# GELU in one ScalarE activation and a second layernorm's rstd on GpSimd, in a gated mix of a long convolution and an MLP mixer

## The chip, the core and the metric

One core of a Trainium2 chip runs the whole program. The metric is the device time of one launch in microseconds (us), from the first to the last instruction and what lies around them; lower is better. PE is the matmul engine (TensorE), PEld its weight loads, ACT is ScalarE, DVE is VectorE, POOL is GpSimd, SP is the engine that here only issues DMAs.

## The reference, cut to what matters

```
x = A_q                                            # 2048 x 640
g = sigmoid((x * gate_w).sum(-1))
a = q * (causal long convolution of kv with ssm_k, by FFT) # kv: 4-tap filter of k, times v
h  = gelu(layernorm(x) @ w1)                       # tanh form, 2048 x 640
hs = (h with its four column groups shifted by 1, -1, 2, -2 rows) @ w2
x1 = x + hs
b  = x1 + gelu(layernorm(x1) @ w3) @ w4            # w3: 640 x 1536, w4: 1536 x 640
out = g * a + (1 - g) * b
```

The GELU is `gelu(x, approximate=True)`, that is x * sigmoid(1.5957691 * (x + 0.044715 x^3)).

## The kernel before, in words

Every operation is recorded by hand in program order (`P.op`, `P.dma`); a small recorder works out from the named reads and writes of each operation which semaphores it must wait for, also on an earlier operation of its own engine (PE's writes excepted). Each engine runs its operations in exactly the order in which the code records them. A helper, `pipeline(stages, n)`, records n items through several stages with the later stages first in each step, so item t is in stage s while item t+1 is in stage s-1.

The program goes through these parts, the times being those of the profiled execution:

- **Loading and first layernorm** (0 to 110 us). 16 tiles of 128 rows: k, v and q are read on SP's queue, DVE makes kv, ACT and DVE make the layernorm, DMA transposes write `xT`. Then 16 gate columns, where ACT's sigmoid (L581) and DVE alternate.
- **mm1, the product with w1** (110 to 157 us, `mm1_s0` at L613). 20 items: 4 chunks of 512 rows, 5 column groups each. An item is 5 matmuls 128x128 by 512 columns into one of the four PSUM banks of `PB` (L619), followed by the GELU of `gelu_stages` (L589): a square on ACT (L595), a multiply-add on DVE (L598), a sigmoid on ACT (L602), a product on DVE (L624). In the fifth item of each chunk the last product is four DVE instructions of 32 partitions each (L637), since each row group lands at another shift. A bank is free for the item four later when the last product has read it.
- **mm2, the product with w2, and the second layernorm** (157 to 209 us, `mm2_s0` at L664). 16 tiles of 128 rows: 10 matmuls of 320 columns, then DVE adds the residual (L686), takes the statistics (L502, L503, L504), ACT takes a square root (L506), DVE the reciprocal (L510), minus mean times rstd (L511) and the normalised tile (L515). SP writes x1 to a scratch tensor, reads the next q and transposes the tile. DVE's order in a step is `ln_dve` of the tile before, then L686 and the statistics of this one; so what follows L504 on DVE is L510 of the same tile.
- **Forward DFT and its pointwise products** (202 to 357 us). Eight units; a unit is 48 matmuls for the filter and kv (L773), evacuated by 24 ACT copies (L776), and then some 27 DVE products (L819 to L835) of about 16 us. The units on PE and ACT run ahead of DVE as far as buffers go.
- **mm3 and mm4** (340 to 479 us). Four chunks of 512 rows. mm3: 12 items of 5 matmuls by 512 columns (L854) into the four banks of `PA`, each with the same GELU; its last product (L860) writes `uT`. mm4: 4 tiles of 24 matmuls by 320 columns (L887), each closed by a DVE instruction (L897). With each tile a row tile of x1 is read back from the scratch tensor and scaled on ACT (L840) for the tile three later.
- **Inverse DFT and output** (479 to 544 us): 448 matmuls of 320 columns (L947), ACT and DVE behind them.

The weights w3 and w4 are loaded by two DMAs of POOL's queue, recorded behind mm2 (L704, L705).

```
    pipeline([mm1_s0, mm1_s1, mm1_s2, mm1_s3, mm1_s4], len(mm1_items))
...
    pipeline([mm2_s0, mm2_s1, mm2_s2, mm2_s3], NT)
```

Of the kernel before, what the change touches and what calls it, by code (L numbers as in the profile page):

```python
# [8 lines left out]
ACTF = mybir.ActivationFunctionType  # L9
ALU = mybir.AluOpType  # L10
# [221 lines left out]
def bass_gated_mix__ssm_conv_h3__mixer_s_mlp__prompt_kernel(  # L232
# [2 lines left out]
    S, D, F = 2048, 640, 1536  # L235
    NT, DC, FC = 16, 5, 12
    T, BLK, NB, NJ = 1024, 512, 4, 4
    GELU_C1 = 0.044715
    GELU_C2 = 1.5957691216057308
    SQC1 = float(np.sqrt(GELU_C1))  # L240

    P = Prog(nc, pools={"sp": ("sp", 20), "sp_out": ("sp", 3), "sp_scr": ("sp", 3), "act": ("act", 8),
                        "pool": ("pool", 8)})
# [57 lines left out]
    oXrel = alloc(3 * 640)  # L301
    oX1rot = alloc(3 * 640)
    oX1rel = alloc(3 * 640)
    oGel = alloc(3 * 3 * 512)
    oJunk = alloc(2 * 640)
    oXn = alloc(3 * 640)
    oQ = oXrel
# [47 lines left out]
    hTv = V(oHT, 5 * HT_W).rearrange("p (c s) -> p c s", c=5)  # L355
# [12 lines left out]
    xrel = [V(oXrel + i * 640, 640) for i in range(3)]  # L368
    x1rot = [V(oX1rot + i * 640, 640) for i in range(3)]
    x1rel = [V(oX1rel + i * 640, 640) for i in range(3)]  # L370
    gel = [[V(oGel + (s * 3 + i) * 512, 512) for i in range(3)] for s in range(3)]
    junk = [V(oJunk + i * 640, 640) for i in range(2)]
    xn = [V(oXn + i * 640, 640) for i in range(3)]
    qt = [V(oQ + i * 640, 640) for i in range(2)]
# [189 lines left out]
    def st2(t):  # L564
# [4 lines left out]
         r=["taps", "Drow"], w=["taps"])  # L569

    GB = 3
    for t in range(NT):
        for c in range(DC):
            P.op("pe", lambda e, t=t, c=c: e.matmul(bankA(GB)[:, t:t + 1], xT[:, c, t * 128:(t + 1) * 128],  # L574
                                                   gwT[:, c:c + 1], start=(c == 0), stop=(c == DC - 1)),
                 r=[("xT", t), "gwT"], w=["gateps", ("bankA", GB)])
    P.op("dve", lambda e: e.tensor_scalar(gsum[:, 1:2], gsum[:, 0:1], -1.0, None, op0=ALU.mult), r=["gsum"], w=["gsum"])
    for t in range(NT):
        P.op("dve", lambda e, t=t: e.tensor_tensor(gcol(t, 2), scol(0, t, 8), gsum[:, 1:2], ALU.mult),
             r=[("stat", 0, t), "gsum"], w=[("gc", t)])  # L580
        P.op("act", lambda e, t=t: e.activation(gcol(t, 0), bankA(GB)[:, t:t + 1], ACTF.Sigmoid,  # L581
                                                bias=gcol(t, 2), scale=scol(0, t, 5)),
             r=["gateps", ("bankA", GB), ("gc", t), ("stat", 0, t)], w=[("gc", t)])
        P.op("dve", lambda e, t=t: e.tensor_scalar(gcol(t, 1), gcol(t, 0), -1.0, 1.0, op0=ALU.mult, op1=ALU.add),
             r=[("gc", t)], w=[("gc", t)])

    gslot = [0]

    def gelu_stages(ps_ap, key_ps, dst_fn):  # L589
        slot = gslot[0] % 3  # L590
        gslot[0] += 1
        sq, z, sg = gel[slot]

        def a1():
            P.op("act", lambda e: e.activation(sq, ps_ap, ACTF.Square, scale=SQC1), r=[key_ps], w=[("gel", slot, 1)])  # L595

        def d1():
            P.op("dve", lambda e: e.scalar_tensor_tensor(out=z, in0=sq, scalar=1.0, in1=ps_ap, op0=ALU.add, op1=ALU.mult),  # L598
                 r=[("gel", slot, 1), key_ps], w=[("gel", slot, 2)])

        def a2():
            P.op("act", lambda e: e.activation(sg, z, ACTF.Sigmoid, scale=GELU_C2), r=[("gel", slot, 2)], w=[("gel", slot, 3)])  # L602

        def d2():
            for (fn, wk) in dst_fn(sg, ps_ap):
                P.op("dve", fn, r=[("gel", slot, 3), key_ps], w=wk)
        return (a1, d1, a2, d2)

    SHIFT = [1, -1, 2, -2]
    mm1_items = [(sc, ft) for sc in range(4) for ft in range(5)]  # L610
    mm1_g = {}

    def mm1_s0(k):  # L613
        sc, ft = mm1_items[k]
        bb = k % 4
        psb = bankB(bb)
        for c in range(DC):
            lhsT = w1v[:, c, 160 * ft:160 * ft + 128] if ft < 4 else w1t4v[:, c, :]
            P.op("pe", lambda e, lhsT=lhsT, c=c, sc=sc, psb=psb: e.matmul(  # L619
                psb, lhsT, xT[:, c, sc * 512:(sc + 1) * 512], start=(c == 0), stop=(c == DC - 1)),  # L620
                 r=["w1"] + [("xT", 4 * sc + i) for i in range(4)], w=[("bankB", bb)])
        if ft < 4:
            def dst_fn(sg, ps_ap, ft=ft, sc=sc):
                return [(lambda e: e.tensor_tensor(hTv[:, ft, 2 + sc * 512:2 + (sc + 1) * 512], sg, ps_ap, ALU.mult),  # L624
                         [("hT", ft, sc)])]
        else:
            offs = ((0, 3), (32, 1), (64, 4), (96, 0))
            wkeys = [("hT", 4, sc)]
# [5 lines left out]
            def dst_fn(sg, ps_ap, sc=sc, wkeys=wkeys):
                lst = []
                for p0, co in offs:
                    lst.append((lambda e, p0=p0, co=co: e.tensor_tensor(  # L637
                        hTv[p0:p0 + 32, 4, co + sc * 512:co + (sc + 1) * 512], sg[p0:p0 + 32, :],
                        ps_ap[p0:p0 + 32, :], ALU.mult), wkeys))
                return lst  # L640
# [5 lines left out]
    def mm1_s2(k):
        mm1_g[k][1]()

    def mm1_s3(k):
        mm1_g[k][2]()  # L650

    def mm1_s4(k):
        mm1_g[k][3]()
# [189 lines left out]
    mm3_g = {}  # L843

    def emit_mm3(sc):
        ub = sc % 2
        uT = uTv[ub]

        def s0(ft):
            k = sc * FC + ft  # L850
            b = k % 4
            psb = bankA(b)
            for c in range(DC):
                P.op("pe", lambda e, psb=psb, c=c, ft=ft: e.matmul(  # L854
                    psb, w3v[:, c, ft * 128:(ft + 1) * 128], xT[:, c, sc * 512:(sc + 1) * 512],
                    start=(c == 0), stop=(c == DC - 1)),
                     r=["w3"] + [("xT", 4 * sc + i) for i in range(4)], w=[("bankA", b)])
# [8 lines left out]
        def s2(ft):
            mm3_g[sc * FC + ft][1]()

        def s3(ft):
            mm3_g[sc * FC + ft][2]()  # L870

        def s4(ft):
            mm3_g[sc * FC + ft][3]()
# [129 lines left out]
```

## Time and profile before

| | us |
|---|---|
| median of 3 runs | 545.34 |
| lowest and highest | 542.97, 547.1 |
| span of the profiled execution, first to last instruction | 544.1 |
| busy: PE, DVE, ACT, POOL | 313.8, 364.8, 213.6, 15.8 |

The profiled execution has no own total beside its span; the median lies 1.2 us above that span, well inside the spread of the three runs. Busy times are sums over the span: no engine is busy all of it, and which one limits changes from part to part, so the parts are read one by one below.

### The profile page before, as it was taken

How to read it: one execution, taken by the hardware profiler on the slowest of the kernel's cores; microseconds unless marked ns; L12 is line 12 of the kernel's file. 1: busy time of each engine (PE TensorE's matmuls, PEld its weight loads, DVE VectorE, ACT ScalarE, POOL GpSimd, SP SyncE). 2: the span in 40 equal slices, each digit the busy share in tenths (PEclk: the TensorE clock that was granted, in tenths of full speed). 3: DMA queues.
4: the chain of work that ended last, by engine and by line, in shares of the span. 5: the costliest groups of instructions: out<-in, count | busy, mean ns of one | idle time of the engine just before them, and what ended most of it. 6: DMA issues, size and time to landing. Idle time of an engine off the chain costs nothing.

```text
span 544.1 us, 5685 instructions
## 1 busy us (share of the span) xinstructions
PE 313.8 (58%) x1809; PEld 173.1 (32%) x1819; DVE 364.8 (67%) x775; ACT 213.6 (39%) x436; POOL 15.8 (3%) x28
## 2 busy tenths in 40 slices
PE   1000000047664467994267406368789798899996
PEld 0000000012232233552123102125445363577774
DVE  1657858738988884999999993985482937432222
ACT  2555434366630004771233204354563818321111
POOL 3110100010000000000000000000000000000000
PEclk9999999997989997998588756769999999999999
DMA  6599999880016663000000000040101010122221
GB/s 185 113 216 270 299 245 260 196 302 0 1 40 156 154 136 96 2 0 1 1 0 0 0 0 2 0 154 14 36 1 48 2 37 12 37 72 74 84 79 56
DMA packets 59114, 46.01 MB, mean 85 GB/s; under 512 B 35136, under 2 KB 57662, under 8 KB 58830
## 3 DMA queue, kind: packets, MB, share of 16 engines
q1 hardware_dynamic: 36062, 31.46, 21.7%
q10 hardware_dynamic: 21152, 5.25, 6.0%
q0 software_dynamic: 1872, 8.96, 4.9%
q8 instruction: 14, 0.23, 0.2%
q14 instruction: 14, 0.11, 0.1%
HBM read 32.54 MB, written 5.24 MB: 69 GB/s over the span
## 4 chain that ended last, share of the span: by engine, by line
DVE 48%; PE 26%; DMA 11%; issue 6%; ACT 5%; SPq 2%; POOL 0%; DVEq 0%; ACTq 0%; POOLq 0%
PE PA L947 11%; PE PB L887 9%; DMA arena<-in_A_k_dram 9%; DVE arena L835 9%; DVE arena L832 7%; DVE arena L860 5%; DVE arena L598 4%; PE PA L773 3%; DVE arena L686 2%; SPq L125 2%; DVE arena L637 2%; PE PB L619 2%; DVE arena L502 1%; DVE arena L503 1%; DVE arena L822 1%
## 5 line engine op out<-in xcount | busy, mean ns | idle before, releaser
L773 PE MATMUL PA<-arena 128*128 128x512 bf16 (+1 forms) x384 | 80.7, 377 | 57.6 <-ACT arena L776 57.6
L776 ACT ACTIVATE arena<-PA 128x512 bf16<-128x512 f32 (+1 forms) x96 | 50.5, 526 | 81.8 <-DVE arena L832 60.6
L773 PEld LDWEIGHTS PA<-arena 128*128 128x128 bf16 x384 | 40.3, 106 | 97.8 <-ACT arena L776 61.4
L854 PE MATMUL PA<-arena 128*128 128x512 bf16 x232 | 56.9, 391 | 23.0 <-DVE arena L860 22.1
L947 PE MATMUL PA<-arena 128*128 128x320 bf16 x448 | 61.0, 299 | 0.0
L887 PE MATMUL PB<-arena 128*128 128x320 bf16 x384 | 54.3, 299 | 5.5 <-DVE arena L860 5.5
L574 PE MATMUL PA<-arena 128*128 128x1 bf16 x80 | 4.7, 169 | 90.3 <-DMA arena<-arena 90.3
L602 ACT ACTIVATE arena<-arena 128x512 bf16<-128x512 bf16 x68 | 42.4, 623 | 21.3 <-DVE arena L598 21.3
L835 DVE TENSOR_TENSOR arena<-arena 128x960 bf16<-128x960 bf16 (+2 forms) x96 | 47.2, 492 | 3.3
L947 PEld LDWEIGHTS PA<-arena 128*128 128x128 bf16 x448 | 43.8, 98 | 17.0
L832 DVE TENSOR_TENSOR arena<-arena 128x960 bf16<-128x960 bf16 (+2 forms) x96 | 46.6, 486 | 0.0
L887 PEld LDWEIGHTS PB<-arena 128*128 128x128 bf16 x384 | 37.2, 98 | 22.5 <-DVE arena L860 7.9
L598 DVE SCALAR_TENSOR_TENSOR arena<-arena,PA 128x512 bf16<-128x512 bf16 x48 | 32.4, 683 | 12.9 <-ACT arena L595 12.9
L854 PEld LDWEIGHTS PA<-arena 128*128 128x128 bf16 x240 | 22.1, 99 | 57.1 <-ACT arena L595 32.8
L677 PE MATMUL PB<-arena 128*128 128x320 bf16 x160 | 24.6, 300 | 25.0 <-DVE arena L686 22.1
L897 DVE SCALAR_TENSOR_TENSOR arena<-PB,arena 128x640 bf16<-128x640 f32 x16 | 14.1, 884 | 36.6 <-PE PB L887 36.6
L962 DVE TENSOR_TENSOR arena<-arena 128x640 bf16<-128x640 bf16 x16 | 7.9, 493 | 45.5 <-ACT arena L956 45.5
L619 PE MATMUL PB<-arena 128*128 128x512 bf16 x98 | 29.2, 454 | 12.7 <-DVE arena L624 6.2
L956 ACT ACTIVATE arena<-PA,arena 128x640 bf16<-128x640 f32 x16 | 12.7, 794 | 54.7 <-PE PA L947 54.7
L860 DVE TENSOR_TENSOR arena<-arena,PA 128x512 bf16<-128x512 bf16 x48 | 32.7, 682 | 0.8
L574 PEld LDWEIGHTS PA<-arena 128*128 128x128 bf16 x80 | 3.4, 106 | 91.6 <-DMA arena<-arena 91.6
L840 ACT ACTIVATE arena<-arena 128x640 bf16<-128x640 bf16 x16 | 13.0, 826 | 45.9 <-DMA arena<-x_scratch 45.9
(88 smaller groups left out, 364.2 us busy)
## 6 DMA issues: line engine op xcount, KB each, us to landing
arena<-in_A_k_dram SPq DMA_DIRECT2D x61, 160.0 KB, 6.2
arena<-in_A_q_dram SPq DMA_DIRECT2D x48, 160.0 KB, 2.6
arena<-in_B_w_dram POOLq DMA_DIRECT2D x2, 1920.0 KB, 10.8
arena<-in_A_v_dram SPq DMA_DIRECT2D x16, 160.0 KB, 6.8
x_scratch<-arena SPq DMA_DIRECT2D x16, 160.0 KB, 1.8
arena<-x_scratch SPq DMA_DIRECT2D x16, 160.0 KB, 2.2
out_dram<-arena SPq DMA_DIRECT2D x16, 160.0 KB, 1.8
arena<-cG POOLq DMA_DIRECT2D x1, 2048.0 KB, 7.8
```

Source lines behind the costliest of these rows:

```text
L598: P.op("dve", lambda e: e.scalar_tensor_tensor(out=z, in0=sq, scalar=1.0, in1=ps_ap, op0=ALU.add, op1=ALU.mult), r=[("gel", slot, 1), key_ ...
L602: P.op("act", lambda e: e.activation(sg, z, ACTF.Sigmoid, scale=GELU_C2), r=[("gel", slot, 2)], w=[("gel", slot, 3)])
L619: P.op("pe", lambda e, lhsT=lhsT, c=c, sc=sc, psb=psb: e.matmul(psb, lhsT, xT[:, c, sc * 512:(sc + 1) * 512], start=(c == 0), stop=(c == D ...
L677: P.op("pe", lambda e, lhsT=lhsT, ft=ft, hh=hh, bk=bks[hh]: e.matmul(bk[:, 0:320], lhsT, w2v[:, ft, hh * 320:(hh + 1) * 320], start=(ft == ...
L773: P.op("pe", lambda e, psb=psb, tc=tc, q0=q0, rhs=rhs, ncol=ncol: e.matmul(psb[:, 0:ncol], Rv[:, tc, q0:q0 + 128], rhs, start=(tc == 0), s ...
L776: P.op("act", lambda e, psb=psb, dst=dst, bb0=bb0, bb1=bb1, dd0=dd0, dd1=dd1, nb_=nb_, ncol=ncol: e.activation(dst[:, bb0:bb1, dd0:dd1], p ...
L832: P.op(eng, lambda e, pt=pt, kvap=kvap, ri_h=ri_h, a=a, nbb=nbb, un=un: e.tensor_tensor(pt[:, 0:nbb, :], kvap, Hbc(ri_h, a, nbb, n=un), AL ...
L835: P.op(eng, lambda e, pt=pt, yap=yap, nbb=nbb, opc=opc: e.tensor_tensor(yap, yap, pt[:, 0:nbb, :], opc), r=[pk, ykey], w=[ykey])
L854: P.op("pe", lambda e, psb=psb, c=c, ft=ft: e.matmul(psb, w3v[:, c, ft * 128:(ft + 1) * 128], xT[:, c, sc * 512:(sc + 1) * 512], start=(c ...
L860: return [(lambda e: e.tensor_tensor(uT[:, ft, :], sg, ps_ap, ALU.mult), [("uT", ub, ft)])]
L887: P.op("pe", lambda e, bk=bk, fcx=fcx, tt=tt, hh=hh: e.matmul(bk[:, 0:320], uT[:, fcx, (tt % 4) * 128:(tt % 4) * 128 + 128], w4v[:, fcx, h ...
L947: P.op("pe", lambda e, bk=bk, fcx=fcx, cc=cc, u0=u0, hh=hh, i=i, n_mm=n_mm: e.matmul(bk[:, 0:320], Gv[:, fcx, u0:u0 + 128], Yv[:, fcx, cc, ...
```

## The change

The four-step GELU (square, multiply-add, sigmoid, product) becomes one ACT instruction with the tanh-form GELU function, which reads the PSUM bank and writes the result where the last product wrote it. In mm1 the fifth item of each chunk needs four such instructions of 32 partitions each. The pipelines of mm1 and mm3 shrink from five stages to two. In the second layernorm the square root on ACT and the reciprocal on DVE go, and two GpSimd instructions on a 128x1 column come: add 1e-5, then raise to the power -0.5. The first layernorm stays as it is.

```
-        P.op("act", lambda e: e.activation(scol(l, t, 5), scol(l, t, 9), ACTF.Sqrt, bias=cst[:, 0:1], scale=1.0),
+
+    def ln_dve(l, t, src_ap, src_key):
+        P.op("pool", lambda e: e.tensor_scalar(scol(l, t, 5), scol(l, t, 9), 1e-5, None, op0=ALU.add),
+             r=[("stat", l, t)], w=[("stat", l, t)])
+        P.op("pool", lambda e: e.tensor_tensor(scol(l, t, 6), scol(l, t, 5), cst[:, 2:3], ALU.pow),
              r=[("stat", l, t), "cst"], w=[("stat", l, t)])
-    def ln_dve(l, t, src_ap, src_key):
-        P.op("dve", lambda e: e.reciprocal(scol(l, t, 6), scol(l, t, 5)), r=[("stat", l, t)], w=[("stat", l, t)])
...
         def a1():
-            P.op("act", lambda e: e.activation(sq, ps_ap, ACTF.Square, scale=SQC1), r=[key_ps], w=[("gel", slot, 1)])
-
-        def d1():
-            P.op("dve", lambda e: e.scalar_tensor_tensor(out=z, in0=sq, scalar=1.0, in1=ps_ap, op0=ALU.add, op1=ALU.mult),
-                 r=[("gel", slot, 1), key_ps], w=[("gel", slot, 2)])
-
-        def a2():
-            P.op("act", lambda e: e.activation(sg, z, ACTF.Sigmoid, scale=GELU_C2), r=[("gel", slot, 2)], w=[("gel", slot, 3)])
-
-        def d2():
-            for (fn, wk) in dst_fn(sg, ps_ap):
-                P.op("dve", fn, r=[("gel", slot, 3), key_ps], w=wk)
-        return (a1, d1, a2, d2)
+            for (dst, src, wk) in dst_fn(ps_ap):
+                P.op("act", lambda e, dst=dst, src=src: e.activation(dst, src, ACTF.Gelu_apprx_tanh), r=[key_ps], w=wk)
+        return (a1,)
...
-    pipeline([mm1_s0, mm1_s1, mm1_s2, mm1_s3, mm1_s4], len(mm1_items))
+    pipeline([mm1_s0, mm1_s1], len(mm1_items))
...
-        pipeline([s0, s1, s2, s3, s4], FC)
+        pipeline([s0, s1], FC)
```

How the instructions stand in the built programs follows for three places. In the program after, line numbers are its own: L578 is the gate's sigmoid (L581 before), L587 the GELU, L743 the DFT's evacuation (L776 before), L504 and L506 the two GpSimd instructions of the second layernorm.

ACT at the start of mm1, before: the gate's sigmoids, then square and sigmoid of the GELU by turns.

```order
L581 ACT_TABLE_LOAD
L581 ACTIVATE arena<-PA,arena 128x1 x16
L595 ACTIVATE arena<-PB 128x512 x2
L602 ACTIVATE arena<-arena 128x512
L595 ACTIVATE arena<-PB 128x512
```

The same place after:

```order
L578 ACT_TABLE_LOAD
L578 ACTIVATE arena<-PA,arena 128x1 x16
L587 ACT_TABLE_LOAD
L587 ACTIVATE arena<-PB 128x512 x4
L587 ACTIVATE arena<-PB 32x512 x4
```

A second table load now stands between the gate and the first GELU, and ACT has 32 GELU instructions in mm1 in place of 20 squares and 20 sigmoids.

ACT from the end of mm1 to the start of the DFT, before:

```order
L595 ACTIVATE arena<-PB 128x512
L602 ACTIVATE arena<-arena 128x512 x2
L506 ACT_TABLE_LOAD
L506 ACTIVATE arena<-arena 128x1 x16
L776 ACTIVATE arena<-PA 128x2x256 x2
L776 ACTIVATE arena<-PA 128x4x64
```

The same place after:

```order
L587 ACTIVATE arena<-PB 32x512 x4
L587 ACTIVATE arena<-PB 128x512 x4
L587 ACTIVATE arena<-PB 32x512 x4
L743 ACTIVATE arena<-PA 128x2x256 x2
L743 ACTIVATE arena<-PA 128x4x64
```

The 16 square roots of mm2 no longer stand between the GELU and the DFT's evacuations, and the table load that they needed is gone.

POOL, whose queue holds the weight loads, before: the constant R of the DFT, then w3 and w4, then the constant G of the inverse DFT.

```order
L125 DMA arena<-in_B_w_dram 32x640 x4
L125 DMA arena<-cR 128x4096
L125 DMA arena<-in_B_w_dram 128x5x1536
L125 DMA arena<-in_B_w_dram 128x12x640
L125 DMA arena<-cG 128x8192
```

The same place after, up to the first tile's two instructions:

```order
L125 DMA arena<-in_B_w_dram 32x640 x4
L125 DMA arena<-cR 128x4096
L504 ISA
L504 TENSOR_SCALAR arena<-arena 128x1
L506 TENSOR_TENSOR arena<-arena 128x1
```

Sixteen such pairs now stand ahead of the loads of w3 and w4, and one ISA instruction, a reload of POOL's library, ahead of the first pair.

## Rows read from the trace of the kernel before

**Rows 1.** The page's chain of work that ended last, shares by engine

```profile
DVE 48%; PE 26%; DMA 11%; issue 6%; ACT 5%; SPq 2%; POOL 0%; DVEq 0%; ACTq 0%; POOLq 0%
```

**Rows 2.** Busy time by stretch: start:end, length, busy us (instructions), PEclk, DMA share, GB/s

```profile
120.00:157.00 37.00, 25.18 (x94) 9.34 (x95) 32.96 (x55) 24.10 (x42) 0.00 (x0) 0.86 0.03 11
385.30:405.00 19.70, 15.39 (x70) 6.17 (x70) 15.50 (x25) 14.72 (x26) 0.00 (x0) 1.00 0.04 10
479.00:544.10 65.10, 60.78 (x448) 43.54 (x446) 16.62 (x33) 12.71 (x16) 0.00 (x0) 1.00 0.25 76
```

**Rows 3.** GELU of mm1, grouped by line and form: busy us, mean ns | idle before

```profile
L598 DVE SCALAR_TENSOR_TENSOR arena<-arena,PB 128x512 bf16<-128x512 bf16 x20 | 13.6, 683 | 3.0 <-ACT arena L595 2.9
L595 ACT ACTIVATE arena<-PB 128x512 bf16<-128x512 f32 x20 | 11.8, 595 | 5.2 <-PE PB L619 4.6
L637 DVE TENSOR_TENSOR arena<-arena,PB 32x512 bf16<-32x512 bf16 x16 | 10.9, 684 | 0.5
L624 DVE TENSOR_TENSOR arena<-arena,PB 128x512 bf16<-128x512 bf16 x16 | 10.9, 682 | 0.1
```

**Rows 4.** Timeline into mm1: start us, us, what, count, [idle before, releaser]

```profile
108.99 1.28 ACT L581 ACT_TABLE_LOAD   x1 [8.24 <-DVE arena L579]
120.25 0.35 ACT L581 ACTIVATE arena<-PA,arena 128x1 f32<-128x1 f32 x1 [0.29 <-DVE arena L579]
123.34 7.01 PE L619 MATMUL PB<-arena 128*128 128x512 bf16 x20 [6.24 <-DVE arena L624]
128.41 1.44 PEld L619 LDWEIGHTS PB<-arena 128*128 128x128 bf16 x7 [0.28 <-issue]
```

**Rows 5.** Timeline of mm2: its first residual add, and the last two tiles

```profile
157.46 0.82 DVE L686 TENSOR_TENSOR arena<-PB,arena 128x640 bf16<-128x640 f32 x1
...
204.67 0.21 DVE L504 BATCH_NORM_AGGREGATE arena<-arena 128x2 f32<-128x12 f32 x1
204.91 0.29 ACT L506 ACTIVATE arena<-arena 128x1 f32<-128x1 f32 x1 [2.94 <-DVE arena L504]
...
205.43 0.16 DVE L511 SCALAR_TENSOR_TENSOR arena<-arena 128x1 f32<-128x1 f32 x1
...
205.99 0.82 DVE L686 TENSOR_TENSOR arena<-PB,arena 128x640 bf16<-128x640 f32 x1
```

**Rows 6.** Timeline from mm2 into the first DFT unit

```profile
201.77 3.19 PE L773 MATMUL PA<-arena 128*128 128x512 bf16 x16
...
208.34 0.58 ACT L776 ACTIVATE arena<-PA 128x512 bf16<-128x512 f32 x1
...
208.86 0.45 DVE L515 TENSOR_SCALAR arena<-arena 128x640 bf16<-128x640 bf16 x1
212.17 0.49 DVE L789 COPY arena<-arena 128x1280 bf16<-128x1280 bf16 x1 [2.86 <-ACT arena L776]
...
213.37 0.59 DVE L791 MEMSET arena<- 1x640 uint32 x1 [0.19 <-DVE arena L790]
217.93 0.82 DVE L819 TENSOR_TENSOR arena<-arena 128x1280 bf16<-128x1280 bf16 x1 [3.97 <-ACT arena L776]
```

**Rows 7.** POOL's groups by line: busy us, mean ns | idle before

```profile
L125 POOL DMA_DIRECT2D arena<-in_A_shift_k_dram x1 | 0.9, 903 | 0.0
L125 POOL DMA_DIRECT2D arena<-in_A_ssm_D_dram x1 | 0.5, 508 | 0.0
L988 POOL MEMSET const-float32-0.0<- 128x1 f32 x1 | 0.1, 98 | 0.2 <-issue 0.2
```

**Rows 8.** Timeline of mm3: its first matmuls, a chunk's start, the end of mm4

```profile
340.05 4.26 PE L854 MATMUL PA<-arena 128*128 128x512 bf16 x19
...
358.85 1.44 PE L854 MATMUL PA<-arena 128*128 128x512 bf16 x3 [14.54 <-DVE arena L860]
...
388.78 0.83 ACT L840 ACTIVATE arena<-arena 128x640 bf16<-128x640 bf16 x1 [2.75 <-DMA arena<-x_scratch]
...
478.77 61.02 PE L947 MATMUL PA<-arena 128*128 128x320 bf16 x448
```

More of the change, by code (lines that the diff above doesn't have):

```diff
@@ L237, in bass_gated_mix__ssm_conv_h3__mixer_s_mlp__prompt_kernel @@
     T, BLK, NB, NJ = 1024, 512, 4, 4
-    GELU_C1 = 0.044715
-    GELU_C2 = 1.5957691216057308
-    SQC1 = float(np.sqrt(GELU_C1))
     P = Prog(nc, pools={"sp": ("sp", 20), "sp_out": ("sp", 3), "sp_scr": ("sp", 3), "act": ("act", 8),
@@ L303, in bass_gated_mix__ssm_conv_h3__mixer_s_mlp__prompt_kernel @@
     oX1rel = alloc(3 * 640)
-    oGel = alloc(3 * 3 * 512)
     oJunk = alloc(2 * 640)
@@ L370, in bass_gated_mix__ssm_conv_h3__mixer_s_mlp__prompt_kernel @@
     x1rel = [V(oX1rel + i * 640, 640) for i in range(3)]
-    gel = [[V(oGel + (s * 3 + i) * 512, 512) for i in range(3)] for s in range(3)]
     junk = [V(oJunk + i * 640, 640) for i in range(2)]
@@ L401, in bass_gated_mix__ssm_conv_h3__mixer_s_mlp__prompt_kernel @@
     P.op("dve", lambda e: e.memset(cst[:, 1:2], 1.0), w=["cst"])
+    P.op("dve", lambda e: e.memset(cst[:, 2:3], -0.5), w=["cst"])
     P.dma("pool", V(oId, 128).bitcast(U16), cI.ap(), w=["ident"])
@@ L585, in bass_gated_mix__ssm_conv_h3__mixer_s_mlp__prompt_kernel @@
              r=[("gc", t)], w=[("gc", t)])
-    gslot = [0]
     def gelu_stages(ps_ap, key_ps, dst_fn):
-        slot = gslot[0] % 3
-        gslot[0] += 1
-        sq, z, sg = gel[slot]
         def a1():
-            P.op("act", lambda e: e.activation(sq, ps_ap, ACTF.Square, scale=SQC1), r=[key_ps], w=[("gel", slot, 1)])
-        def d1():
-            P.op("dve", lambda e: e.scalar_tensor_tensor(out=z, in0=sq, scalar=1.0, in1=ps_ap, op0=ALU.add, op1=ALU.mult),
-                 r=[("gel", slot, 1), key_ps], w=[("gel", slot, 2)])
-        def a2():
-            P.op("act", lambda e: e.activation(sg, z, ACTF.Sigmoid, scale=GELU_C2), r=[("gel", slot, 2)], w=[("gel", slot, 3)])
-        def d2():
-            for (fn, wk) in dst_fn(sg, ps_ap):
-                P.op("dve", fn, r=[("gel", slot, 3), key_ps], w=wk)
-        return (a1, d1, a2, d2)
+            for (dst, src, wk) in dst_fn(ps_ap):
+                P.op("act", lambda e, dst=dst, src=src: e.activation(dst, src, ACTF.Gelu_apprx_tanh), r=[key_ps], w=wk)
+        return (a1,)
     SHIFT = [1, -1, 2, -2]
@@ L622, in mm1_s0, with dst_fn @@
         if ft < 4:
-            def dst_fn(sg, ps_ap, ft=ft, sc=sc):
-                return [(lambda e: e.tensor_tensor(hTv[:, ft, 2 + sc * 512:2 + (sc + 1) * 512], sg, ps_ap, ALU.mult),
-                         [("hT", ft, sc)])]
+            def dst_fn(ps_ap, ft=ft, sc=sc):
+                return [(hTv[:, ft, 2 + sc * 512:2 + (sc + 1) * 512], ps_ap, [("hT", ft, sc)])]
         else:
@@ L632, in mm1_s0, with dst_fn @@
                 wkeys.append(("hT", 4, sc + 1))
[L634 to L640, printed above, removed]
+            def dst_fn(ps_ap, sc=sc, wkeys=wkeys):
+                return [(hTv[p0:p0 + 32, 4, co + sc * 512:co + (sc + 1) * 512], ps_ap[p0:p0 + 32, :], wkeys)
+                        for p0, co in offs]
         mm1_g[k] = gelu_stages(psb, ("bankB", bb), dst_fn)
@@ L644, in mm1_s1 @@
         mm1_g[k][0]()
[L646 to L653, printed above, removed]
-    pipeline([mm1_s0, mm1_s1, mm1_s2, mm1_s3, mm1_s4], len(mm1_items))
+    pipeline([mm1_s0, mm1_s1], len(mm1_items))
     P.handoff(["shk"], ["bnbuf"])
@@ L857, in s0, with dst_fn3 @@
                      r=["w3"] + [("xT", 4 * sc + i) for i in range(4)], w=[("bankA", b)])
-            def dst_fn3(sg, ps_ap, ft=ft):
-                return [(lambda e: e.tensor_tensor(uT[:, ft, :], sg, ps_ap, ALU.mult), [("uT", ub, ft)])]
+            def dst_fn3(ps_ap, ft=ft):
+                return [(uT[:, ft, :], ps_ap, [("uT", ub, ft)])]
             mm3_g[k] = gelu_stages(psb, ("bankA", b), dst_fn3)
@@ L864, in s1 @@
             mm3_g[sc * FC + ft][0]()
[L866 to L873, printed above, removed]
-        pipeline([s0, s1, s2, s3, s4], FC)
+        pipeline([s0, s1], FC)
     def emit_mm4(sc):
```

## The prediction

> **What bounds the kernel now.** I read the chain of work that ended last first. DVE holds 48% of it and PE 26% [rows 1], so a change that takes work from DVE can count, where DVE is what ends last. The busy times by stretch say where that is. In mm1 DVE is busy 32.96 of 37 us, PE 25.18, at a granted clock of 0.86; in mm3 DVE is busy 15.50 of 19.70 us and PE 15.39; in the inverse DFT PE is busy nearly all the time (60.78 of 65.10) at full clock [rows 2]. The groups by line give the price of the GELU: on DVE a multiply-add of 683 ns and a product of 682 ns for each item, and four of 684 ns in each fifth item [rows 3]. For mm1 that is 20 x 0.683 + 16 x 0.682 + 16 x 0.684 = 35.5 us of DVE: the bound. The timelines then show the seams, where one part hands over to the next [rows 4 to 6, 8]. One per cent, about 5 us, is what a measurement of this kernel tells from no change.
>
> **mm1.** ACT ends the last gate sigmoid at 120.25 + 0.35 = 120.6, where the four banks have long been full [rows 4]. The GELU's table load comes now, on the path: 1.28 us, as the sigmoid's load at 108.99 took, so 121.9. The GELU itself stands in no row. It reads 128x512 f32 from PSUM and writes bf16 as the square of L595 does, 595 ns [rows 3]; its bounds are the 0.58 us of a plain copy of that shape [rows 6] and twice the square, 1.2 us; I take 0.6, the value of the nearest row. So the first bank is free at 122.5, against 123.34 for PE's restart before [rows 4]. Twenty of the 100 matmuls are done by then. Before, PE came back from 6.24 us of idling at the lower clock: its weight loads were spread out until 128.41, 5.1 us after the restart, and close-packed from there [rows 4]. That is 1.2 GHz at first, then 2.4. I keep those 5.1 us. The full-clock price of a 512-column matmul is 4.26 us / 19 = 0.224 [rows 8], twice that at half the clock, so 11 to 12 matmuls go in the slow part and 68 are left: 15.2 us. PE is done at 122.5 + 5.1 + 15.2 = 142.8. ACT has 32 instructions x 0.6 = 19.2 us from 121.9 on, just beside PE's 20.3; PE remains the later one, and four banks cover a fifth item's four instructions. The first mm2 tile adds 10 x 60.78/448 = 1.4 us [rows 2], so the first residual add starts at 144.2 in place of 157.46 [rows 5]: 13.3 us won.
>
> The Trainium skill's page "ScalarE: Activation LUTs" (section "What ACT_TABLE_LOAD costs") says that a switch of sets costs the load and a drain, 2.66 us together. The row shows the 1.28 us alone; by the page the sum would be 1.4 us higher.
>
> **mm2.** Its 16 tiles follow one another at (205.99 - 157.46)/15 = 3.235 us, and DVE sets that pace: the ACT root between L504 and L510 is waited for in DVE's own order. From the end of L504 (204.88) to the start of L511 (205.43) go 0.55 us [rows 5]. After the change two POOL instructions fill that gap, and DVE's L511, L515 and the next tile's L686 are all queued behind the second of them. POOL runs no arithmetic in this trace. From below, two constant fills of 98 ns and three hand-overs of 0.03 us (204.88 to 204.91, L504 to ACT): 0.3 us. From above, two of POOL's longest single instructions, 903 ns, with hand-overs: 1.9 us [rows 7]. A constant fill reads nothing and computes nothing, so the nearest row is POOL's shortest instruction that does work in software, 508 ns: 2 x 0.508 + 0.1 = 1.1 us. A tile becomes 0.55 us longer, 3.785; the ends are 0.25 less and 1.35 more. Fifteen tiles: the last residual add starts at 144.2 + 56.8 = 201.0, against 205.99. So mm2 gives 8.3 us of the 13.3 back (between -3.8 and 20.3 at the ends).
>
> POOL's library reload, recorded ahead of the first pair, has all of mm1's time to itself; I cost it at nothing. Without that cover its nearest row is ACT's load of 1.28 us. The Trainium skill's "GPSIMD Engine Reference" (section 2.1, Instruction dispatch) says that the first call to a freshly loaded kernel pays about 6 us of instruction load that no row shows; no run here shows it so far, and paid in the first tile it would make the sum 6 us higher.
>
> The loads of w3 and w4 move behind the POOL pairs, to about 205 us. mm3 needs them at 329, so the DFT hides them.
>
> **The seam into the DFT.** PE had done the first unit's 16 matmuls that fit into four banks by 205, but ACT evacuated the first bank only at 208.34, directly behind the last square root; L819, the first long product, started at 217.93, 11.94 us after the last residual add [rows 5, 6]. With the roots gone ACT can evacuate at once. PE begins the unit behind tile 15, which waits for the residual add two tiles back: 2 x 3.785 - 0.85 - 1.5 = 5.2 us before the last one. At the rate of the row (16 in 3.19 us) the unit's 48 matmuls take 9.6 us, and one evacuation 0.6: 5.0 us after the last residual add. DVE is later: L515 ends 3.3 us after that add now, 3.9 with the slower rstd, and the three copies (212.17 to 213.96) add 1.8: L819 starts 5.7 us after it. That wins 6.2 us more; none if PE's clock falls in mm2. L819 at 206.7 in place of 217.93. From there to mm3's first matmul nothing changes: 340.05 - 217.93 = 122.1 us, so 328.8.
>
> **mm3 and mm4.** Before, PE filled four banks at 340.05 and then stood 14.54 us, because DVE took up the GELU only behind its DFT products; later chunks go at DVE's pace [rows 2, 8]. Now the GELU needs no DVE. ACT's 12 x 0.6 = 7.2 us lie beside a chunk's 60 x 0.224 = 13.4 us of PE; PE is late next. PE's work is 240 x 0.224 + 384 x 60.78/448 = 53.8 + 52.1 = 105.9 us [rows 2, 8]. One wait stays at each of three chunk borders: ACT stands in its order behind the scaling of the tile of x1 that the last L897 releases, which ends at 388.78 + 0.83 = 389.6, with one GELU 390.2 [rows 8]. PE's four banks last from 385.3 to 385.3 + 20 x 0.224 = 389.8. So 0.4 to 0.5 us, 1.5 for three. Sum 107.4 against 478.77 - 340.05 = 138.7 before: 31.3 us won. DVE's products in the first chunk are no obstacle. They end one multiply-add, sigmoid and product (some 2.1 us) ahead of 358.85, so 16.7 us after mm3's start, and mm4's first tile asks for DVE at 13.4 + 24 x 60.78/448 = 16.7 us.
>
> **Sum.** 328.8 + 107.4 = 436.2, and the tail of 544.1 - 478.77 = 65.3 us as before: a span of 501.5, 42.6 less than 544.1 (13.3 - 8.3 + 6.2 + 31.3, rounded). The median of the runs lies 1.2 us over the span, which gives 502.7; I say 502.
>
> **The rivals.**
> *GpSimd's power is slow, and the kernel ends slower.* If the power is worked out by a long routine for each element, DVE waits for it 16 times. The price decides from 1.1 + 42.6/16 = 3.8 us for the pair on; at 4.5 us the time is 502 + 16 x 3.4 = 556. For it: no row prices a power. Against it: the longest single POOL instruction here takes 0.9 us, and the column has one element per partition. 6%.
> *The pair is quick.* At 0.3 us mm2 becomes faster than before: 502 - 16 x 0.8 = 489. For it the fills of 98 ns. 20%.
> *The GELU takes twice a square.* ACT then bounds: mm1 32 x 1.2 = 38 us, some 17 us worse than forecast, and mm3 12 x 1.2 = 14.4 us a chunk plus a last GELU uncovered, 4 x 1.6: 502 + 17 + 6.5 = 525. Against it: square and copy of that shape agree, at 0.595 and 0.58 us [rows 3, 6]. 5%.
> *PE keeps the lower clock in mm1.* Its granted clock there was 0.86 [rows 2]; if it never rises, 68 x 0.224 = 15 us more: 517. Against it: PE would be packed closer than before. 8%.
> *The DFT's first unit runs at the lower clock* since tiles in mm2 leave PE idle longer: the seam wins nothing, 508. 8%.
>
> **How the numbers follow.** The forecast keeps 53%. The quick pair reaches down to 489, and a little over the sum of both good ends gives 486. Upwards the 1.9 us bound gives 502 + 13 = 515, the slow clock 517, and two smaller mishaps together 522. Outside lie the slow power, the doubled GELU and some of the tails, under 2 in 10. All cases but the slow power are faster by over 1%: 92%; within 1% there is only a pair near 3.8 us, 2%; slower 6%.
>
> **What would show it right or wrong.** mm3's matmuls in one piece from their first to the inverse DFT, with waits under 1 us at the borders; the first residual add near 144; mm2's tiles 3.8 us apart and POOL's two instructions filling the gap behind L504; the first L819 under 6 us after the last residual add; GELU rows of 0.6 us; w3 landing long before mm3. Wrong, if a tile of mm2 takes over 6 us, if ACT has no idle time in mm1 while PE waits for it, or if PE waits in mm3 for anything other than the x1 tile.

## The result, and the profile after

The kernel after the change takes 500.62 us in the median (495.56 to 502.61, 4 runs), the kernel before on the same chip 546.21 (542.97 to 547.1): a ratio of 0.9158, 95% interval 0.9095 to 0.9221. The forecast was 502. A few executions of a kernel come out over 1.5% above its fastest; the ratios here and below leave these out, the medians do not.

The chain of work that ended last in the kernel after, by engine, answers to [rows 1]: DVE gave up 8 points of it, PE gained 5, and POOL is on it for the first time.

```profile
DVE 40%; PE 31%; DMA 14%; ACT 4%; issue 4%; POOL 3%; SPq 2%; DVEq 0%; ACTq 0%; POOLq 0%
```

Busy time by stretch (start:end, length, then busy us of PE, PEld, DVE, ACT and POOL, granted clock, DMA share, GB/s): mm1 as a whole, then its start behind PE's restart and its rest by themselves; mm2; the DFT's first unit; mm3 with mm4.

```profile
124.00:147.00 23.00, 21.04 (x90) 9.53 (x92) 0.13 (x1) 18.32 (x32) 0.00 (x0) 0.85 0.00 1
125.90:130.60 4.70, 4.69 (x12) 1.66 (x13) 0.00 (x0) 3.67 (x7) 0.00 (x0) 0.50 0.00 0
130.60:145.70 15.10, 15.05 (x71) 6.92 (x71) 0.00 (x0) 11.56 (x21) 0.00 (x0) 1.00 0.00 0
147.00:204.60 57.60, 36.85 (x192) 19.55 (x190) 40.15 (x94) 5.88 (x11) 11.95 (x31) 0.82 0.50 123
197.20:206.10 8.90, 8.90 (x52) 4.83 (x50) 5.74 (x15) 5.82 (x11) 2.63 (x7) 1.00 0.39 92
329.30:435.50 106.20, 103.90 (x616) 60.73 (x623) 28.68 (x45) 39.91 (x66) 0.56 (x1) 1.00 0.14 44
```

Against [rows 2], DVE has gone from mm1 (0.13 of 23 us), where PE now holds the pace with ACT close beside it. In mm3 and mm4 PE is busy 103.90 of 106.20 us, so only 2.3 us of waiting are left there. In mm2 DVE is busy only 40.15 of 57.60 us, and PE's granted clock is 0.82 over this stretch. In mm2 of the kernel before it was 1.00:

```profile
157.50:206.00 48.50, 25.26 (x161) 14.57 (x161) 40.48 (x106) 4.41 (x15) 0.00 (x0) 1.00 0.57 142
```

The groups by line show the new instructions (busy us, mean ns, then the idle time before them and what ended it).

```profile
L587 ACT ACTIVATE arena<-PA 128x512 bf16<-128x512 f32 x48 | 27.0, 595 | 14.0 <-PE PA L821 14.0
L506 POOL TENSOR_TENSOR arena<-arena 128x1 f32<-128x1 f32 x16 | 9.1, 568 | 1.3
L587 ACT ACTIVATE arena<-PB 128x512 bf16<-128x512 f32 x16 | 8.8, 599 | 1.9 <-PE PB L600 1.9
L504 POOL TENSOR_SCALAR arena<-arena 128x1 f32<-128x1 f32 x16 | 3.5, 222 | 120.0 <-DVE arena L500 120.0
L508 DVE SCALAR_TENSOR_TENSOR arena<-arena 128x1 f32<-128x1 f32 x16 | 2.6, 160 | 15.9 <-POOL arena L506 15.9
```

The GELU takes what a square took (595 and 599 ns against 595 of L595 in [rows 3]). The last row says where the price of the rstd is paid: DVE's L508 waits 15.9 us for POOL, 16 times 1.0. Root and reciprocal took 0.55 us in that place [rows 5].

The timeline of the kernel after, from the gate into mm1, answers to [rows 4].

```profile
123.60 0.35 ACT L578 ACTIVATE arena<-PA,arena 128x1 f32<-128x1 f32 x1 [0.29 <-DVE arena L576]
123.96 1.28 ACT L587 ACT_TABLE_LOAD   x1
125.26 2.06 ACT L587 ACTIVATE arena<-PB 128x512 bf16<-128x512 f32 x4
125.91 19.78 PE L600 MATMUL PB<-arena 128*128 128x512 bf16 x79 [6.04 <-ACT arena L587]
```

The table load stands on the path, and the GELU begins 0.02 us behind it. PE then runs mm1 to its end without a break. The whole row of times is 3.35 us later than before (123.95 against 120.60 for the gate's end), which has nothing to do with the change: in the nine profiled executions of this study, whose instructions up to there do the same work, the gate ends between 120.6 and 124.0.

The timeline of mm2's first and last tiles and of the seam answers to [rows 5, 6, 7].

```profile
147.09 0.82 DVE L653 TENSOR_TENSOR arena<-PB,arena 128x640 bf16<-128x640 f32 x1 [22.96 <-PE PB L644]
149.31 0.23 POOL L504 TENSOR_SCALAR arena<-arena 128x1 f32<-128x1 f32 x1 [77.96 <-DVE arena L500]
149.63 0.57 POOL L506 TENSOR_TENSOR arena<-arena 128x1 f32<-128x1 f32 x1
...
197.19 14.98 PE L740 MATMUL PA<-arena 128*128 128x512 bf16 x81
198.25 0.60 ACT L743 ACTIVATE arena<-PA 128x512 bf16<-128x512 f32 x1 [50.07 <-PE PA L740]
202.28 0.82 DVE L653 TENSOR_TENSOR arena<-PB,arena 128x640 bf16<-128x640 f32 x1
204.19 0.21 DVE L500 BATCH_NORM_AGGREGATE arena<-arena 128x2 f32<-128x12 f32 x1
204.49 0.22 POOL L504 TENSOR_SCALAR arena<-arena 128x1 f32<-128x1 f32 x1 [2.80 <-DVE arena L500]
204.79 0.57 POOL L506 TENSOR_TENSOR arena<-arena 128x1 f32<-128x1 f32 x1
205.39 0.16 DVE L508 SCALAR_TENSOR_TENSOR arena<-arena 128x1 f32<-128x1 f32 x1 [0.99 <-POOL arena L506]
207.94 0.83 DVE L786 TENSOR_TENSOR arena<-arena 128x1280 bf16<-128x1280 bf16 x1
```

From the end of the statistics (204.40) to L508 go 0.99 us: 0.09 to reach POOL, 0.22 for the addition, 0.08 between the two, 0.57 for the power, 0.03 back. ACT takes up the DFT's first evacuation at 198.25, 4 us ahead of the last residual add; before, it came 2.35 us behind that add. Before, PE stood with four full banks for 4.02 us, and came back at the lower clock. Its first matmuls then, and the stretch up to 213.96 by itself, with a granted clock of 0.51:

```profile
208.98 5.37 PE L773 MATMUL PA<-arena 128*128 128x512 bf16 x15 [4.02 <-ACT arena L776]
```

```profile
208.98:213.96 4.98, 4.98 (x14) 2.08 (x15) 1.90 (x4) 3.06 (x6) 0.00 (x0) 0.51 0.56 140
```

So the old seam was made of two things: ACT came late, and PE, having waited for it, ran the next 5 us at half its clock. The two borders of mm3 and mm4, after the change:

```profile
329.32 6.85 PE L821 MATMUL PA<-arena 128*128 128x512 bf16 x31
...
435.50 1.79 PE L905 MATMUL PA<-arena 128*128 128x320 bf16 x12
```

The parts by their borders in the two timelines, in us (each border is the start of the first instruction of the next part; the gate's end is that of its last sigmoid). The forecast of mm1's length is from the gate's end to the first add, 144.2 - 120.6.

| part | before | forecast | after |
|---|---|---|---|
| up to the gate's end | 120.60 | 120.60 | 123.95 |
| mm1, to the first residual add | 36.86 | 23.6 | 23.14 |
| mm2, first to last residual add | 48.53 | 56.8 | 55.19 |
| seam, to the first long DFT product | 11.94 | 5.7 | 5.66 |
| DFT, to mm3's first matmul | 122.12 | 122.1 | 121.38 |
| mm3 and mm4, to the inverse DFT | 138.72 | 107.4 | 106.18 |
| tail | 65.33 | 65.3 | 65.30 |
| span | 544.1 | 501.5 | 500.8 |

### The profile page after: what moved, and what is told of

Same layout as the page of the kernel before. It is cut to its first block, busy times and chain, and to the rows that moved or that the text cites. A ratio compares the mean times of both kernels' runs of the same rounds, so it can differ in the third digit from the quotient of the medians.

```text
span 500.8 us, 5285 instructions
## 1 busy us (share of the span) xinstructions
PE 307.9 (61%) x1809; PEld 176.7 (35%) x1819; DVE 270.7 (54%) x612; ACT 177.2 (35%) x363; POOL 28.6 (6%) x60
## 3 DMA queue, kind: packets, MB, share of 16 engines
q1 hardware_dynamic: 36062, 31.46, 23.6%
## 4 chain that ended last, share of the span: by engine, by line
DVE 40%; PE 31%; DMA 14%; ACT 4%; issue 4%; POOL 3%; SPq 2%; DVEq 0%; ACTq 0%; POOLq 0%
PE PA L905 12%; DVE arena L802 9%; DVE arena L799 8%; PE PB L845 8%; DMA arena<-in_A_k_dram 8%; PE PA L821 5%; PE PB L600 4%; DMA arena<-x_scratch 3%; DVE arena L653 3%; DMA arena<-in_A_v_dram 2%; POOL arena L506 2%; SPq L125 2%; DVE arena L498 2%; DVE arena L499 2%; PE PA L740 1%
## 5 line engine op out<-in xcount | busy, mean ns | idle before, releaser
L740 PE MATMUL PA<-arena 128*128 128x512 bf16 (+1 forms) x384 | 78.6, 371 | 53.5 <-ACT arena L743 53.5
L743 ACT ACTIVATE arena<-PA 128x512 bf16<-128x512 f32 (+1 forms) x96 | 50.5, 526 | 131.3 <-PE PA L740 65.9
L821 PE MATMUL PA<-arena 128*128 128x512 bf16 x232 | 51.9, 379 | 2.3 <-ACT arena L587 1.9
L845 PE MATMUL PB<-arena 128*128 128x320 bf16 x384 | 52.8, 299 | 0.0
L799 DVE TENSOR_TENSOR arena<-arena 128x960 bf16<-128x960 bf16 (+2 forms) x96 | 46.6, 485 | 0.0
L644 PE MATMUL PB<-arena 128*128 128x320 bf16 x160 | 31.1, 354 | 20.8 <-DVE arena L653 20.2
L845 PEld LDWEIGHTS PB<-arena 128*128 128x128 bf16 x384 | 37.6, 98 | 15.2
L587 ACT ACTIVATE arena<-PA 128x512 bf16<-128x512 f32 x48 | 27.0, 595 | 14.0 <-PE PA L821 14.0
L807 ACT ACTIVATE arena<-arena 128x640 bf16<-128x640 bf16 x16 | 12.8, 824 | 46.6 <-DMA arena<-x_scratch 46.6
L600 PE MATMUL PB<-arena 128*128 128x512 bf16 x98 | 25.4, 425 | 6.3 <-ACT arena L587 6.0
L644 PEld LDWEIGHTS PB<-arena 128*128 128x128 bf16 x160 | 16.6, 111 | 35.2 <-DVE arena L653 26.0
L475 ACT ACTIVATE arena<-arena 128x640 bf16<-128x640 bf16 x16 | 11.8, 735 | 42.3 <-issue 18.9
```

What stands on the lines that cost most here:

```text
L587: P.op("act", lambda e, dst=dst, src=src: e.activation(dst, src, ACTF.Gelu_apprx_tanh), r=[key_ps], w=wk)
L644: P.op("pe", lambda e, lhsT=lhsT, ft=ft, hh=hh, bk=bks[hh]: e.matmul(bk[:, 0:320], lhsT, w2v[:, ft, hh * 320:(hh + 1) * 320], start=(ft == ...
L740: P.op("pe", lambda e, psb=psb, tc=tc, q0=q0, rhs=rhs, ncol=ncol: e.matmul(psb[:, 0:ncol], Rv[:, tc, q0:q0 + 128], rhs, start=(tc == 0), s ...
L743: P.op("act", lambda e, psb=psb, dst=dst, bb0=bb0, bb1=bb1, dd0=dd0, dd1=dd1, nb_=nb_, ncol=ncol: e.activation(dst[:, bb0:bb1, dd0:dd1], p ...
L799: P.op(eng, lambda e, pt=pt, kvap=kvap, ri_h=ri_h, a=a, nbb=nbb, un=un: e.tensor_tensor(pt[:, 0:nbb, :], kvap, Hbc(ri_h, a, nbb, n=un), AL ...
L821: P.op("pe", lambda e, psb=psb, c=c, ft=ft: e.matmul(psb, w3v[:, c, ft * 128:(ft + 1) * 128], xT[:, c, sc * 512:(sc + 1) * 512], start=(c ...
```

## The experiments

**The GELU alone.** The root on ACT and the reciprocal on DVE stay.

```
+        P.op("act", lambda e: e.activation(scol(l, t, 5), scol(l, t, 9), ACTF.Sqrt, bias=cst[:, 0:1], scale=1.0), ...)
     def ln_dve(l, t, src_ap, src_key):
-        P.op("pool", ... 1e-5 ... ALU.add ...)
-        P.op("pool", ... ALU.pow ...)
+        P.op("dve", lambda e: e.reciprocal(scol(l, t, 6), scol(l, t, 5)), ...)
```

> The one-instruction GELU with the second layernorm's square root (ACT) and reciprocal (DVE) kept as in the kernel before. Theory (the parts add, and the rstd change is a draw: it costs 0.44 us a tile in mm2, 6.7 us in all, and wins 6.3 us at the seam into the DFT): mm2 tiles back at 3.24 us, the seam from the last residual add to the first long DFT product back at 11.9 us, mm1 and mm3/mm4 as after the whole change (23.1 and 106.2 us), time about 500 us. Rival (keeping the root costs two more table switches on the path and the seam was not the root's): seam 5.7 us, or a wait of over 2 us for ACT at mm3's start; 494 us by the first, 503 by the second.

Measured: 502.65 us (497.51 to 504.27), ratio to before 0.9208, interval 0.9131 to 0.9286: it can't be told from the whole change. Its parts: mm1 23.65, mm2 48.77 (tiles 3.25), seam 11.38, mm3 and mm4 106.06 us. So, as far as these runs can tell, the whole gain is the GELU's (its one instruction and the shorter pipelines that come with it, which no run separates), and what mm2 wins back (6.4 us) the seam loses (5.7). Two table loads come back with the root: its own, ahead of the first root in mm2, and the GELU's a second time, at mm3's start (columns as in the timelines above):

```profile
329.49 2.26 ACT L806 ACTIVATE arena<-arena 128x640 bf16<-128x640 bf16 x3
331.76 1.28 ACT L586 ACT_TABLE_LOAD   x1
333.05 1.09 ACT L586 ACTIVATE arena<-PA 128x512 bf16<-128x512 f32 x2
```

The second costs next to nothing: PE has four banks to fill meanwhile and then waits 0.47 us, and mm3 with mm4 takes 106.06 us in place of 106.18. The rival is out.

**The rstd alone**, on the kernel before.

```
-        P.op("act", ... ACTF.Sqrt ...)
     def ln_dve(l, t, src_ap, src_key):
-        P.op("dve", lambda e: e.reciprocal(scol(l, t, 6), scol(l, t, 5)), ...)
+        P.op("pool", ... 1e-5 ... ALU.add ...)
+        P.op("pool", ... ALU.pow ...)
```

> The GpSimd rstd alone, on the kernel before with its four-step GELU. Theory: mm2 tiles 3.68 us in place of 3.24 (+6.7 us), the seam 5.7 us in place of 11.9 (-6.3 us), the rest as before: 546 to 547 us, no difference that can be measured. Rival (the pair on POOL is a plain loss, the seam opens only because the GELU lets the parts ahead of it move): 552 to 553 us with the seam near 12.

Measured: 548.15 us (10 runs) against 548.1 before (13 runs), ratio 1.0022, interval 0.9976 to 1.0069. mm2 55.17, seam 6.10 us. Loss and gain cancel, as forecast; this half of the change moves 6 us twice and leaves the time where it was, and the rival, a seam near 12 us, is out. Here PE was still at half clock when it began the DFT's first unit at 209.86 (granted 0.50 from 195 to 210.7, then 1.00), and the seam is 0.4 us longer than in the kernel after.

**A probe for the seam**: an ACT copy that nobody reads, where the root stood.

```
+        P.op("act", lambda e: e.activation(scol(l, t, 10), scol(l, t, 9), ACTF.Copy), r=[("stat", l, t)], w=[("probe", t)])
```

> The kernel after, with one more ACT copy of a 128x1 column behind each tile's statistics, which nobody reads; it holds ACT's queue where the square root held it, and leaves rstd on GpSimd. Theory (the seam is ACT's order): tiles stay at 3.68 us, the seam goes from 5.7 to between 11 and 12 us, the time up by about 6 us to 506. Rival (the seam is owed to the later loads of w3 and w4 or to the longer tiles): seam stays below 6.5 us, the time at 500 to 501.

Measured: 513.82 us (510.12 to 514.47), ratio to before 0.9415, interval 0.9349 to 0.9481. The seam is 12.37 us, a little over the forecast, with rstd on POOL and w3 and w4 loaded late: it was ACT's order, and the rival is out. The time of 506 was missed: the total rose by 13 us and not by 6, since tiles did not stay at 3.68 us but took 4.01. The timeline of the last tile shows why:

```profile
207.27 0.21 DVE L500 BATCH_NORM_AGGREGATE arena<-arena 128x2 f32<-128x12 f32 x1
207.51 0.20 ACT L502 ACTIVATE arena<-arena 128x1 f32<-128x1 f32 x1 [3.77 <-DVE arena L500]
207.74 3.17 ACT L744 ACTIVATE arena<-PA 128x512 bf16<-128x512 f32 x5
207.87 0.22 POOL L505 TENSOR_SCALAR arena<-arena 128x1 f32<-128x1 f32 x1 [3.10 <-ACT arena L502]
208.39 13.97 PE L741 MATMUL PA<-arena 128*128 128x512 bf16 x61 [5.54 <-ACT arena L744]
```

POOL waits for ACT: my probe reads the tile's statistics under the name that POOL's addition writes, so the recorder made the addition wait for the copy, and POOL's start slid from 0.09 to 0.39 us behind L500. That is 0.33 us a tile, 5 us in all, of the probe's own making. And PE stood 5.54 us with four full banks, as it stood 4.02 before, and again came back at half clock (granted 0.50 from 208.39 to 213.4).

**The power without the addition**; the epsilon of the second layernorm is left out.

```
-        P.op("pool", ... 1e-5 ... ALU.add ...)
-        P.op("pool", lambda e: e.tensor_tensor(scol(l, t, 6), scol(l, t, 5), cst[:, 2:3], ALU.pow), ...)
+        P.op("pool", lambda e: e.tensor_tensor(scol(l, t, 6), scol(l, t, 9), cst[:, 2:3], ALU.pow), ...)
```

> The kernel after without the GpSimd addition of 1e-5: the power reads the variance itself (the epsilon of the second layernorm is left out). Theory (each POOL instruction pays its own time and hand-over on DVE's path): the gap from the statistics' end to DVE's next instruction falls from 0.99 to 0.69 us, tiles from 3.68 to 3.38, 4.8 us less in all. Rival (the cost is in reaching POOL and back, whatever it runs): the gap falls by under 0.1 us.

Measured in a single run: 496.02 us, which lies among the times of the kernel after and says little by itself. The tiles took 3.345 us, and the gap is:

```profile
162.42 0.21 DVE L500 BATCH_NORM_AGGREGATE arena<-arena 128x2 f32<-128x12 f32 x1
162.71 0.55 POOL L504 TENSOR_TENSOR arena<-arena 128x1 f32<-128x1 f32 x1 [2.79 <-DVE arena L500]
163.29 0.16 DVE L506 SCALAR_TENSOR_TENSOR arena<-arena 128x1 f32<-128x1 f32 x1 [0.66 <-POOL arena L504]
```

0.66 us in place of 0.99: the addition cost its 0.22 us and a hand-over, on DVE's path, 16 times. That is the theory's 0.69 within 0.03, and the rival is out. Most of what is left is the power itself, 0.55 us.

**The wait covered.** The pair is recorded behind the statistics, and DVE's use of it one tile later. The same shift was made with the root and the reciprocal, and a third kernel also delays the load of the inverse DFT's matrix G.

```
-    pipeline([mm2_s0, mm2_s1, mm2_s2, mm2_s3], NT)
+    pipeline([mm2_s0, mm2_s1, lambda t: None, mm2_s2, mm2_s3], NT)
... (in the third kernel)
-    P.dma("pool", V(oG, 8192).bitcast(U16), cG.ap()..., w=["G"])
+    P.dma("pool", V(oG, 8192).bitcast(U16), cG.ap()..., r=[("Bp", 4)], w=["G"])
```

> The kernel after with the GpSimd pair recorded right behind a tile's statistics and DVE's use of it one tile later (an empty stage in mm2's pipeline), so that DVE has a whole tile of work in between. Theory (the 1.0 us of POOL is paid only because DVE has nothing else in its order): gap gone, tiles 2.7 us in place of 3.68, mm2 40.5 us in place of 55.2; the seam is then PE's and a little longer, about 7.1 us in place of 5.7, since PE starts the DFT unit only 3 us before the last add; 487 to 488 us. Rival (PE, DMA or the tile buffers set the pace once DVE is free, or POOL's port slows DVE): tiles stay above 3.2 us, 493 us or more.

> The one-instruction GELU with the square root and reciprocal kept, and DVE's use of the root one tile later. Theory: tiles 2.88 us (the reciprocal stays on DVE), the seam 11.4 us or a little more, for ACT still stands behind the last root: about 495 us, so 7 to 8 us slower than the covered GpSimd pair, which now is worth its place. Rival (the draw between root and GpSimd remains whatever the order): within 2 us of the covered pair.

> The same with the load of the inverse DFT's matrix (2 MB) made to wait until DVE has closed the fifth tile of mm4. Theory (that load, started when the DFT's products end, held up the read-back of x1 for the first chunk border): the read-back's longest wait falls from 12.4 us to below 6, PE's wait at the first border from 1.4 to 0.5 us or less, about 1 us off the kernel with the covered pair: 486 to 487 us. Rival (the read-back is late since its tile is freed late): the wait at the first border stays above 1.2 us.

| kernel | us (4 runs) | ratio to before, interval | tile | mm2 | seam | mm3 and mm4 |
|---|---|---|---|---|---|---|
| covered GpSimd pair | 483.74 (480.87 to 488.07) | 0.8831, 0.8756 to 0.8907 | 2.51 | 37.61 | 6.76 | 106.38 |
| covered root | 493.44 (488.66 to 497.04) | 0.8961, 0.8874 to 0.9047 | 2.69 | 40.35 | 11.38 | 105.98 |
| covered pair, G late | 484.66 (483.55 to 485.15) | 0.8831, 0.8799 to 0.8862 | 2.51 | 37.61 | 6.76 | 105.26 |

One tile of the covered pair:

```profile
160.81 0.22 POOL L502 TENSOR_SCALAR arena<-arena 128x1 f32<-128x1 f32 x1 [1.67 <-DVE arena L508]
161.12 0.57 POOL L504 TENSOR_TENSOR arena<-arena 128x1 f32<-128x1 f32 x1
161.15 0.82 DVE L653 TENSOR_TENSOR arena<-PB,arena 128x640 bf16<-128x640 f32 x1
162.00 0.49 DVE L498 BATCH_NORM_STATS2 arena<-arena 128x6 f32<-128x320 bf16 x1
162.53 0.49 DVE L499 BATCH_NORM_STATS2 arena<-arena 128x6 f32<-128x320 bf16 x1
163.05 0.21 DVE L500 BATCH_NORM_AGGREGATE arena<-arena 128x2 f32<-128x12 f32 x1
163.18 0.10 DVE L508 SCALAR_TENSOR_TENSOR arena<-arena 128x1 f32<-128x1 f32 x1
163.32 0.45 DVE L512 TENSOR_SCALAR arena<-arena 128x640 bf16<-128x640 bf16 x1
163.68 0.82 DVE L653 TENSOR_TENSOR arena<-PB,arena 128x640 bf16<-128x640 f32 x1
```

POOL still takes 0.57 us for the power, but it lies beside the next tile's residual add, and DVE runs its tile without a gap. The tile is even 0.2 us shorter than I expected: L508 starts 0.08 us before L500 ends and takes 0.10 in place of 0.16. That, 15 times, is most of why the time lies below the 487 to 488 us of the forecast. In this order the GpSimd pair is worth its place: each run of the covered root (488.66 and up) is slower than each of the covered pair (488.07 and down), and the traces place 2.7 us of that in mm2, where the reciprocal stays, and 4.6 in the seam. Together these are 7.4 us, as was forecast (7 to 8). The medians differ by 9.7; in the two traces the rest is the scatter of the loading part, mm1 and the DFT. The rivals are out: the pace is not PE's or the buffers', L653 takes 0.82 us with POOL busy beside it as it does alone, and the draw does not last. PE's granted clock in mm2 is back at 1.00 in this order.

The late G did what was expected of PE. Its waits in mm3, of the covered pair first and then with G late (us in total, times, longest):

```profile
PE PA L821 <- ACT arena L587: 2.1, 3, 1.1
```

```profile
PE PA L821 <- ACT arena L587: 1.0, 3, 0.4
```

mm3 and mm4 take 1.1 us less. The medians don't show it (484.66 and 483.74): the loading part ahead of mm1 differs by more between executions. One forecast was missed: the longest wait for a tile of x1 fell to 6.4 us and not below 6, for a reason given in the last section. Both kernels beat the kernel after by some 16 us.

## Why the prediction was right, point by point

- **mm1.** Forecast 13.3 us won, measured 13.7 (36.86 - 23.14). The GELU's 0.6 us, the exposed table load and the second start of PE at the lower clock all came as worked out: 19.78 us for the stretch of 79 recorded matmuls against 20.3. The start at the lower clock (0.50) lasted 4.7 us against 5.1; from 130.6 on PE had the full clock (1.00), so the rival of a lasting low clock is out. The 35.5 us that the prediction gives as DVE's work before adds instructions that overlap; [rows 2] has 32.96 us busy, and no later sum uses it.
- **The table load and GpSimd's first call.** The Trainium skill's page "ScalarE: Activation LUTs" (section "What ACT_TABLE_LOAD costs") adds a drain of 1.38 us to each load. The rows differ: 1.28 us of load between a sigmoid that ended at 123.95 and a GELU that began at 125.26. The measurement decides, for this place. The 6 us of a first call from the Trainium skill's page "GPSIMD Engine Reference" (section 2.1, Instruction dispatch) were not on the path either: the first pair took 0.23 and 0.57 us, like the last. Whether they were paid in POOL's 78 us of idling ahead of it no run shows.
- **mm2.** Forecast 8.3 us given back, measured 6.7. The term was the pair at 2 x 0.508 + 0.1 = 1.1 us; it measured 0.99. That is near in part by luck, because misses cancel: the addition took 0.22 us, less than half of its price, the power 0.57 and the hand-overs to POOL 0.09 and 0.08 (not 0.03), each more. The rival of a slow power needed 3.8 us, the quick one 0.3; neither came.
- **The seam.** Forecast 5.7 us, measured 5.66, for the reason given: the probe that puts an ACT instruction back where the root stood opens it again. PE ran the DFT's first unit at full clock (1.00 from 197.2 to 206.1), although the clock over mm2 fell from 1.00 to 0.82; the rival of a cold first unit did not come, though PE's clock in mm2 is lower as it feared. With rstd alone the unit did begin at half clock, for 0.85 us, and the seam lost 0.4 us; whether a whole unit at that clock would have cost the 6 us of the prediction, no run shows. What the prediction did not say is that part of the old seam was PE's clock: the 5 us at half clock from 208.98 on cost some 2.5 us (an estimate, half of that stretch). A unit has 12 evacuations by ACT (96 of L743 for eight units), not the 24 given ahead of the prediction; no sum uses that number.
- **mm3 and mm4.** Forecast 31.3 us won, measured 32.5: 103.90 us of PE where I had 105.9, since 0.224 us a matmul was read from a burst of 19 that carries its own ending (68 weight loads of mm1 at full clock follow one another at 14.62 us / 68 = 0.215). Of the three border waits of 0.5 us the first was 1.41 and the other two together 0.5. So one of the prediction's signs, waits under 1 us at the borders, did not come; the cause, a load that it had not looked at, is in the last section.
- **The sum.** From the gate's end on the kernel won 46.6 us (13.7 - 6.7 + 6.3 + 0.7 + 32.5, the 0.7 in the DFT), the forecast had 42.6. In the profiled execution the loading part took 3.35 us more and brought the span back onto the forecast, so the forecast of the span looks better than its terms: against an equal loading part it was some 4 us too high, mostly in mm2 and in mm3 with mm4.

What the prediction did not say, though its own terms showed it, is that the rstd half (8.3 given back, 6.2 won) is not worth making as it stands. That its price is only one of order, the covered pair showed.

## What to carry to other kernels

Ask of a chain of elementwise steps between two matmuls which engine's order it sits in: folding it into one ScalarE instruction was worth 46 us here because it took DVE out of two parts that PE could fill alone. The round trip to GpSimd cost its whole length only because DVE had nothing queued ahead of the answer; recording DVE's use of it one tile later took 1.17 us off a tile, somewhat more than the trip itself. And a short instruction on an engine with little to do, as the root on ACT, can still cost 6 us when the next part's first instructions stand behind it in that engine's order.

## What the runs showed of the hardware that was not expected

A GpSimd power on a 128x1 column took 0.57 us and an addition 0.22, with 0.08 to 0.09 us to start each and 0.03 back to DVE.

A 2 MB load delayed the small reads that started beside it. Timeline of the kernel after at the first chunk border:

```profile
346.58 0.56 POOL L125 DMA_DIRECT2D arena<-cG  x1 [138.68 <-DVE arena L802]
346.85 10.95 SPq L125 DMA_DIRECT2D arena<-x_scratch  x4
...
355.25 2.27 ACT L807 ACTIVATE arena<-arena 128x640 bf16<-128x640 bf16 x3 [12.40 <-DMA arena<-x_scratch]
...
360.98 5.35 PE L821 MATMUL PA<-arena 128*128 128x512 bf16 x24 [1.41 <-ACT arena L587]
```

The first of these 160 KB tiles of x1, issued at 346.85, let ACT go at 355.25, 8.4 us later, where others take 2.2 us to land (the page's median). With G held back the same read, issued at 330.31, let ACT go after 2.4 us:

```profile
330.31 9.73 SPq L125 DMA_DIRECT2D arena<-x_scratch  x4
...
332.75 0.83 ACT L807 ACTIVATE arena<-arena 128x640 bf16<-128x640 bf16 x1 [6.43 <-DMA arena<-x_scratch]
```

So the 6 us by which ACT's wait fell (12.40 to 6.43) are all the read's own; the 4.0 us that are left beside it pass in both before the read is issued, and they are why the wait did not fall below 6. PE's wait at the first border fell from 1.1 us in the covered pair (1.41 in the kernel after) to 0.4. Before the change G was issued at 357.31 and the reading back of x1 went on only at 376.49, so the two did not meet (G's landing took 7.8 us); now mm4 is running when G is loaded.
